# Queries and the first MLP layer in four column strips of the array, with one gelu and whole-array transposes

## The chip, the cores and the metric

The kernel runs on one core of one Trainium2 chip. The metric is the device time of one execution in microseconds (us), as a median of several. Each run is labelled fast or slow. All runs compared here are fast, except one single look (called contiguous below), whose state is unknown, and which is used only for the lengths of some matmuls.

"TensorE", "VectorE", "ScalarE" and "SyncE" are four engines of the core; in lines of the profile they are PE, DVE, ACT and SP. SPq is SyncE's queue, which here issues all the large loads, strictly in order.

## The reference

The result is one step of decoding: attention of 8 sequences over a cache, plus an MLP, plus the input.

```python
# B=8, Sq=1, D=640, H=32 heads (queries and K/V), Sk=4096, Dh=128, F=1728; all bf16
xn  = layernorm(x)
q   = (xn @ wq).reshape(B, 1, 32, 128)                 # wq: 640 x 4096
o   = softmax(q @ k_cache^T * Dh**-0.5) @ v_cache      # k_cache, v_cache: 8 x 32 x 4096 x 128
h   = gelu(layernorm(xn) @ w1 + b1)                    # w1: 640 x 1728, gelu by tanh
out = x + o.reshape(B, 1, 4096) @ wo + h @ w2 + b2
```

The two caches are 2 x 268 MB; all weights together are 14.9 MB. Everything is read once.

## The kernel before

The work is cut into 64 tiles: four heads of one sequence each, with 4.19 MB of K and 4.19 MB of V. There are two K buffers and two V buffers in SBUF. Tiles count from 0 here, loads in words: the first K is that of tile 0, the fifth K that of tile 4.

Every instruction has a position, and each engine executes its own in that order. Waits follow from what an instruction reads and writes. wq, w1 and the hidden layer `h` borrow the space of the two V buffers ("arena"):

```python
arena = KV_sb[:, NK:NK + NV, :]...          # the two V buffers
wq_sb, w1_sb, h_sb, b1_sb = ...             # all inside arena
# ... cut ...
for t in range(T):                          # T = 64
    pos = (-100.0, -98.0)[t] if t < NK else t - 1.5            # K of tile t
    ld(pos, kview(t), A_k_cache ..., [("K", t % NK, q) ...])
    pos = (0.45, 1.2)[t] if t < NV else t + 0.6                # V of tile t
    R = (["wqfree"], ["wqfree", "w1free", "hfree"])[t] if t < NV else []
    ld(pos, vview(t), A_v_cache ..., [("V", t % NV, q) ...], R)
```

So SyncE issues K0, wq, K1, w1, w2 at once. V0 waits until the queries have read wq. K2 waits until buffer 0 has been read. V1 waits until the hidden layer has been transposed out of the arena. K3 stands behind V1.

The two stages that the change rewrites, one matmul output of 8 rows at a time:

```python
def queries(n):                              # n = 0..7, four heads each
    def pe(e):                               # 5 matmuls 8 x 512
        for kc in range(DC):
            i = e.matmul(TRF[0:B, it.box[0], 0:HT * P], xnT_sb[:, 0, kc, :], wq_sb[:, kc, s], ...)
    add("pe", pos, pe, R=["wq", "xT0"], W=[it, "wqfree"], X=[it])
    add("act", pos + .01, lambda e: e.activation(qrow, TRF[0:B, ...], ACT.Copy), ...)     # 8 x 512
    def pe_t(e):                             # 4 transposes of 8 x 128
        for a in range(HT): i = e.transpose(...)
    # ... cut: copy into qT_sb ...

def hidden(n):                               # n = 0..3, 432 columns each
    def pe(e):
        for kc in range(DC):
            e.matmul(TRF[0:B, it.box[0], 0:FW], xnT_sb[:, 1, kc, :], w1_sb[:, kc, s], ...)
        return e.matmul(TRF[0:B, ...], ones_bf[0:1, 0:B], b1_sb[:, s], start=False, stop=True)
    add("act", pos + .001, ... e.activation(h_sb[:, s], TRF[0:B, ...], ACT.Gelu_apprx_tanh) ...)

def hidden_t():                              # 14 small transposes, two copies; W=[..., "hfree"]
    for j in range(FC):
        e.transpose(TR_ps[...], h_sb[:, j:FC * P:FC], ident_bf[0:B, 0:B])
# ... cut ...
add("pe", 1.04, pe_mlp2, ...)                # second MLP layer, 28 matmuls
add("dve", 1.94, ... xb2 += mlp ...)         # its sum, ahead of tile 2's work (2.0 on)
add("pe", c - 0.715, ... transpose of the row maxima ...)   # first softmax (c = 2): 1.285
```

The scores of a tile are made in two ways at once: a quarter of the keys on TensorE (transpose, copy, matmul), three quarters on VectorE, in two halves, each a product, a half-width sum and a reduction.

## Time and profile before

| | before |
|---|---|
| time, median of the first three runs | 1294.43 us (1293.76 to 1295.58) |
| profiled span | 1292.5 us |
| DMA rate from 100 to 1280 us | 431 GB/s |
| VectorE busy | 87% of the span |
| second V issued | 64.88 us |
| last V byte, then end of the span | 1287.94 us, 4.6 us later |

First the page of the kernel before: the span, the rate of the DMA in 40 equal slices (32 us each), and the chain of waits that ended last by engine.

```profile
span 1292.5 us, 19701 instructions
...
GB/s 406 412 413 429 427 434 432 432 426 433 432 433 433 426 431 433 432 429 428 433 433 430 433 426 435 430 433 430 431 430 433 429 431 431 433 428 432 425 437 338
...
DMA 77%; PE 10%; DVE 8%; issue 3%; ACT 1%; SPq 0%; DVEq 0%
...
```

The rate is the same everywhere but in the first three slices and the last. The chain is mostly DMA. This kernel waits for memory, and an improvement has to be looked for where memory waits for the kernel.

The same in chosen stretches. The columns are the stretch, its length, then busy us of PE, PEld, DVE, ACT and POOL with instruction counts, the granted clock of TensorE, the busy share of the DMA engines, and GB/s.

```profile
...
core 0: us, PE busy (x) PEld busy (x) DVE busy (x) ACT busy (x) POOL busy (x), PEclk, DMA share, GB/s
...
64.00:68.00 4.00, 3.60 (x24) 2.11 (x24) 0.30 (x1) 0.31 (x2) 0.00 (x0) 0.58 0.73 256
60.00:80.00 20.00, 12.87 (x107) 7.27 (x106) 13.09 (x8) 9.60 (x27) 0.00 (x0) 0.76 0.93 387
...
84.00:88.00 4.00, 2.24 (x30) 0.78 (x18) 3.96 (x2) 0.60 (x1) 0.00 (x0) 0.86 0.93 393
...
100.00:1280.00 1180.00, 591.28 (x7244) 376.07 (x7248) 1047.48 (x519) 460.59 (x1157) 0.00 (x0) 0.54 1.00 431
...
```

From 64 to 68 us the rate falls to 256 GB/s. The cause is in SyncE's issues, in order of time (start, length, what; x2 are two loads merged into one row, the second issued at the end of it, 84.07 us):

```profile
...
43.38 0.34 SPq L365 DMA_DIRECT2D KV_sb<-in_A_v_cache_dram  x1
47.77 0.33 SPq L365 DMA_DIRECT2D KV_sb<-in_A_k_cache_dram  x1
64.88 0.33 SPq L365 DMA_DIRECT2D KV_sb<-in_A_v_cache_dram  x1
65.25 19.18 SPq L365 DMA_DIRECT2D KV_sb<-in_A_k_cache_dram  x2
```

and in what SyncE waited for in the first 110 us (total, times, longest):

```profile
...
SPq L365 <- PE TR_ps L718: 16.8, 1, 16.8
...
```

The last transposes of the hidden layer (line 718) held the second V back by 16.8 us, and the fourth K stood behind it.

And the end, on TensorE: the last 32 value matmuls, which start when the last V piece has landed, and the output projection. Then two microseconds of the end in the table of stretches (the granted clock is the third number from the right).

```profile
...
1287.98 0.65 PE L626 MATMUL PV_ps<-KV_sb,P_sb 128*4 128x128 bf16 x32 [0.45 <-DMA KV_sb<-in_A_v_cache_dram]
...
1289.50 0.45 PE L665 MATMUL TR_ps<-wo_sb,oTn_sb 128*8 128x160 bf16 x16 [0.26 <-DVE oTn_sb L657]
```

```profile
...
1288.00:1290.00 2.00, 1.26 (x49) 0.78 (x49) 0.17 (x1) 0.28 (x1) 0.00 (x0) 1.00 0.00 0
...
```

The clock is 1.00 there (0.85 on the mean of the two microseconds before), and the 32 matmuls take 0.65 us.

### The profile page before, as it was taken

The numbers are of one execution on the slowest core, as the hardware profiler recorded it, in microseconds if no ns is written. First come the engines' busy times: TensorE is split into PE (matmuls) and PEld (weight loads), VectorE is DVE, ScalarE is ACT, GpSimd is POOL, SyncE is SP. The second block draws the span as 40 slices with busy tenths as digits, with TensorE's granted clock in tenths as the row PEclk, the third lists the DMA queues.
The fourth block names the chain that finished last, engine by engine and source line by source line (L and its number), as shares of the span: only waits on it lengthen the run. The fifth ranks groups of instructions, "written<-read, shape, count | busy, mean of one in ns | idle before, by whom it ended". The sixth has DMA issues, their size and how long they took to land.

```text
span 1292.5 us, 19701 instructions
## 1 busy us (share of the span) xinstructions
PE 653.1 (51%) x7852; PEld 407.0 (31%) x7853; DVE 1121.9 (87%) x586; ACT 500.6 (39%) x1248; POOL 0.2 (0%) x4
## 2 busy tenths in 40 slices
PE   2764454554454455454445444444544554455456
PEld 0343233333233233233233232232332332333332
DVE  4979999998898888998988988988888988889885
ACT  1553444334344234343243442443432443433432
POOL 0000000000000000000000000000000000000000
PEclk9865655555555555555555555655555555555566
DMA  9999999999999999999999999999999999999997
GB/s 406 412 413 429 427 434 432 432 426 433 432 433 433 426 431 433 432 429 428 433 433 430 433 426 435 430 433 430 431 430 433 429 431 431 433 428 432 425 437 338
DMA packets 23519, 551.99 MB, mean 427 GB/s; under 512 B 2297, under 2 KB 6481, under 8 KB 6482
## 3 DMA queue, kind: packets, MB, share of 16 engines
q1 hardware_dynamic: 23472, 551.80, 99.6%
q8 instruction: 7, 0.11, 0.0%
q10 hardware_dynamic: 34, 0.02, 0.0%
q14 instruction: 6, 0.05, 0.0%
HBM read 551.80 MB, written 0.01 MB: 427 GB/s over the span
## 4 chain that ended last, share of the span: by engine, by line
DMA 77%; PE 10%; DVE 8%; issue 3%; ACT 1%; SPq 0%; DVEq 0%
DMA KV_sb<-in_A_v_cache_dram 76%; PE PV_ps L616 8%; DVE Y_sb L544 4%; DVE Y_sb L548 2%; DMA KV_sb<-in_A_wq_dram 2%; DVE S_sb L551 1%; PE TR_ps L452 1%; PE TR_ps L704 0%; ACT KT_sb L515 0%; PE PV_ps L731 0%; ACT qrow_sb L456 0%; PE TR_ps L512 0%; PE TR_ps L705 0%; PE CH_ps L565 0%; PE S_ps L522 0%
## 5 line engine op out<-in xcount | busy, mean ns | idle before, releaser
L544 DVE TENSOR_TENSOR Y_sb<-KV_sb,qbc_sb 128x6144 bf16<-128x6144 bf16 x128 | 429.0, 3352 | 86.7 <-DMA KV_sb<-in_A_k_cache_dram 70.6
L551 DVE TENSOR_REDUCE S_sb<-Y_sb 128x48 f32<-128x3072 bf16 x128 | 429.2, 3353 | 4.4
L515 ACT ACTIVATE KT_sb<-TR_ps 128x1024 bf16<-128x1024 bf16 x256 | 254.3, 1019 | 223.6 <-PE TR_ps L512 222.1
L616 PE MATMUL PV_ps<-KV_sb,P_sb 128*16 128x512 bf16 x2040 | 226.8, 624 | 139.9 <-DMA KV_sb<-in_A_v_cache_dram 139.9
L512 PE MATMUL TR_ps<-ident_bf,KV_sb 128*128 128x128 bf16 x2048 | 247.4, 307 | 68.6 <-DMA KV_sb<-in_A_k_cache_dram 68.6
L548 DVE TENSOR_TENSOR Y_sb<-Y_sb 128x3072 bf16<-128x3072 bf16 x128 | 225.0, 1758 | 4.4
L512 PEld LDWEIGHTS TR_ps<-ident_bf,KV_sb 128*128 128x128 bf16 x2048 | 199.5, 141 | 79.2 <-DMA KV_sb<-in_A_k_cache_dram 73.1
L522 PE MATMUL S_ps<-qk_sb,KT_sb 128*128 128x4 bf16 x2048 | 98.2, 170 | 139.7 <-ACT KT_sb L515 138.0
L635 ACT ACTIVATE E_sb<-PV_ps 128x512 bf16<-128x512 f32 (+1 forms) x65 | 38.5, 592 | 319.9 <-PE PV_ps L616 318.4
L616 PEld LDWEIGHTS PV_ps<-KV_sb,P_sb 128*16 128x16 bf16 x2040 | 62.6, 124 | 253.0 <-DMA KV_sb<-in_A_v_cache_dram 145.5
L522 PEld LDWEIGHTS S_ps<-qk_sb,KT_sb 128*128 128x128 bf16 x2048 | 86.4, 109 | 170.5 <-ACT KT_sb L515 170.5
L583 ACT ACTIVATE P_sb<-S_sb,NB_sb 32x128 bf16<-32x128 f32 x256 | 101.9, 398 | 3.8
L641 PE MATMUL C_ps<-sel_bf,E_sb 128*128 128x4 bf16 x256 | 17.0, 172 | 135.4 <-DVE rinv_sb L597 112.4
L577 ACT ACTIVATE NB_sb<-CH_ps 128x2 f32<-128x2 f32 (+1 forms) x33 | 5.7, 172 | 167.1 <-PE CH_ps L573 167.1
L565 PE MATMUL CH_ps<-ident_f,M_sb 128*2 128x128 f32 (+1 forms) x33 | 12.1, 366 | 109.9 <-DVE M_sb L563 109.9
L641 PEld LDWEIGHTS C_ps<-sel_bf,E_sb 128*128 128x128 bf16 x256 | 11.5, 104 | 167.0 <-DVE rinv_sb L597 111.5
L532 ACT ACTIVATE S_sb<-S_ps 32x32 f32<-32x32 f32 x256 | 48.1, 188 | 32.2 <-PE S_ps L522 30.0
L583 ACT ACTIVATION_READ_ACCUMULATOR P_sb<-S_sb,NB_sb 32x1 f32 x256 | 47.0, 184 | 0.0
L565 PEld LDWEIGHTS CH_ps<-ident_f,M_sb 128*2 128x2 f32 (+1 forms) x33 | 2.6, 80 | 112.8 <-DVE M_sb L563 112.6
L656 DVE MEMSET oTn_sb<- 128x16 uint32 x31 | 2.2, 72 | 31.1 <-PE ACC_ps L676 31.1
L567 DVE TENSOR_REDUCE M_sb<-CH_ps 2x4 f32<-2x128 f32 (+1 forms) x33 | 9.2, 279 | 21.6 <-PE CH_ps L565 21.6
L594 PEld LDWEIGHTS C_ps<-rs_sb,ones_f 128*128 128x128 f32 x64 | 13.8, 269 | 25.1 <-issue 21.7
(91 smaller groups left out, 218.4 us busy)
## 6 DMA issues: line engine op xcount, KB each, us to landing
KV_sb<-in_A_k_cache_dram SPq DMA_DIRECT2D x64, 4096.0 KB, 26.8
KV_sb<-in_A_v_cache_dram SPq DMA_DIRECT2D x63, 4096.0 KB, 35.2
KV_sb<-in_A_wq_dram SPq DMA_DIRECT2D x1, 5120.0 KB, 24.1
wo_sb<-in_A_wo_dram SPq DMA_DIRECT2D x8, 640.0 KB, 30.9
KV_sb<-in_B_w_dram SPq DMA_DIRECT2D x1, 2160.0 KB, 38.0
w_sb<-in_B_w_dram SPq DMA_DIRECT2D x1, 2080.0 KB, 42.8
KV_sb<-in_A_v_cache_dram SPq DMA_DIRECT2D x1, 2048.0 KB, 12.6
KV_sb<-in_A_v_cache_dram SPq DMA_DIRECT2D x2, 1024.0 KB, 15.1
```

The source lines that it names most:

```text
L512: r = e.transpose(TR_ps[:, it.box[0], jj * P:(jj + 1) * P], kv[:, n * BK + jj, :], ident_bf[:, :])
L515: add("act", t - 0.59 + 0.12 * n, lambda e: e.activation(KT_sb[:, m % NS, :, :].rearrange("p a b -> p (a b)"), TR_ps[:, it.box[0], :], ACT ...
L522: r = e.matmul(S_ps[:, c:c + HT], KT_sb[:, m % NS, jj, :], qk_sb[:, :, i], start=True, stop=True)
L532: r = e.activation(S_sb[s, g % SR, i, 0:JP], S_ps[s, 0:JP * HT].rearrange("p (j a) -> p j a", a=HT)[:, :, a], ACT.Copy)
L544: return e.tensor_tensor(y, kv[:, j0:j1, :], qbc_sb[:, g % 2, i, :][:, None, :].to_broadcast([P, nj, P]), ALU.mult)
L548: lambda e, y=y, y2=y2: e.tensor_tensor(y2, y[:, :, 0:P // 2], y[:, :, P // 2:P], ALU.add),
L551: lambda e, y2=y2, j0=j0, j1=j1: e.tensor_reduce(S_sb[:, g % SR, i, j0:j1], y2, AX.X, ALU.add),
L565: add("pe", c - 0.715, lambda e: e.transpose(M1T_ps[0:n, :], M1_sb[:, 0:n], ident_f[:, :]), R=["M1", "identf"], W=["M1T"], X=["CH"])
L583: r = e.activation(P_sb[s, i, :, a, :], S_sb[s, g % SR, i, :].rearrange("p (m c) -> p m c", c=4), ACT.Exp, bias=NB_sb[s, g % 2, i:i + 1], ...
L616: r = e.matmul(PV_ps[32 * ct:32 * ct + HT * 4, t % 2, :], P_sb[:, i, m, :, :].rearrange("p a c -> p (a c)"), vv[:, 4 * m:4 * m + 4, :].rea ...
L635: add("act", pos, lambda e: e.activation(E_sb[:, k, 0:n], PV_ps[:, k, 0:n], ACT.Copy), R=[("PV", k)] + ["wo"] * (t % GT), W=[("E", k)], X= ...
L641: r = e.matmul(OT_i, E_sb[:, t % 2, c * P:(c + 1) * P], sel_bf[:, c:HT * 4:4], start=(c == 0), stop=(c == 3 and not last))
```

## The change

The intent is to use all of TensorE's array where only 8 of its 128 columns were used. Four heads of queries go to four strips of 32 output partitions in one PSUM tile, so one eviction of 128x128 and one whole transpose replace an eviction of 8x512 and four transposes. The hidden layer goes into four strips likewise: one gelu of 128x512 for four of 8x432, and four whole transposes for 14 small ones. To give the second layer its layout, the matmuls now read w1 three elements at a time in steps of 13.

```diff
 def pe(e):                                                       # queries
+    q = TRF[:, it.box[0], 0:P]
+    e.matmul(q, zeros_bf[:, :], zeros_bf[:, :], start=True, stop=False, ...)
     for kc in range(DC):
-        i = e.matmul(TRF[0:B, it.box[0], 0:HT * P], xnT_sb[:, 0, kc, :], wq_sb[:, kc, s], ...)
+        for a in range(HT):
+            h = n * HT + a
+            i = e.matmul(q[32 * a:32 * a + B, :], xnT_sb[:, 0, kc, :], wq_sb[:, kc, h * P:(h + 1) * P], ...)
...
-    for a in range(HT):
-        i = e.transpose(TR_ps[:, it2.box[0], a * B:(a + 1) * B], qrow[:, a * P:(a + 1) * P], ident_bf[0:B, 0:B])
+    e.transpose(TR_ps[:, it2.box[0], 0:P], qrow, ident_bf[:, :])
...
-for n in range(FB):
-    hidden(n)                                                    # 6 matmuls and a gelu each
-hidden_t()
+w13 = w1_sb[:, :, 0:FC * P].rearrange("p c (f u) -> p c f u", u=FC)
+for k in range(FB):
+    yield k, 0, FS, w13[:, :, :, 3 * k:3 * k + 3], ...           # 384 columns, strip k
+yield 0, FS, FS + P, w13[:, :, :, FC - 1], ...                   # 128 columns, strip 0
+yield 1, FS, FS + FR, w1_sb[:, :, FC * P:F], ...                 # 64 columns, strip 1
...
+e.matmul(h, zeros_bf[:, :], ...)                                 # zero, then 36 matmuls
+e.activation(h_sb, TRF[:, it_h.box[0], :], ACT.Gelu_apprx_tanh)  # one gelu, 128 x 512
+for c in range(3):
+    e.transpose(TR_ps[:, it_t.box[0], c * P:(c + 1) * P], h_sb[:, c:FS:3], ident_bf[:, :])
```

The order of the loads is not touched.

## The prediction

> **What bounds the kernel now: the DMA queue, almost everywhere.** The busy table of stretches gives a mean DMA share of 1.00 at 431 GB/s from 80 to 1280 us; 551.8 MB at that rate are 1280 us of the 1292.5 us span. The chain that ended last is 77% DMA. VectorE (87% busy) needs 2 x (3.35 + 1.76 + 3.35) = 16.9 us per tile, whose K and V take 8.39 MB / 431 GB/s = 19.5 us to load: slack. Time can only come from DMA holes, or from the 4.6 us tail after the last V byte (1287.9 us), which the change leaves alone.
>
> **Where the DMA starves.** By 20 us stretches: 401 (start latency), 416, 421, 387 GB/s, then about 431. The hole is at 64 to 67 us (107, 229, 262 GB/s): everything queued (18.05 MB at start, first V, third K: 26.4 MB, dry at about 63 us) was used up while the second V tile waited at the head of SyncE's in-order queue for the hidden-layer transposes (that wait: 16.8 us; issued 64.88 us). Against 431 GB/s, 60 to 80 us lost 0.88 MB, 2.0 us; 62 to 68 alone lost 1.3 us. A small loss (0.3 us) lies at 44 to 48 us, where the first V was issued at 43.38 us, just as the queue ran out.
>
> **Costs of the change.**
> - Queries, before: groups 3 to 7 repeat every 1.92 us: five 8x512 matmuls 1.26, eviction 0.59, semaphores. After: one zeroing matmul and 20 matmuls 8x128 in four strips. The trace's own strip matmuls give the rate: 32 of 16x512 in 3.59 us, 112 ns each against a 427 ns pitch unpacked (first query group); 32 of 4x128 in 0.65 us. The Trainium skill (TensorEngine Tiling, Theoretical Speedup: up to 4x for a dimension up to 32) agrees: 3.8x here. Estimate: matmuls 0.55, eviction of 128 columns 0.29 (as the 128x128 eviction at 1288.7), 0.95 us per group. Queries end near 36 us, not 44.3.
> - Hidden layer, before: 55.23 to 65.2 us. After: zeroing 0.43, six passes of 384 + 128 columns, about 0.43 each at the low clock, one gelu 0.6 for four of 0.52, four transposes 0.4, one copy 0.3: about 5 us. The weights are now read in 26-byte steps; the Trainium skill (SBUF — State Buffer, Specifications: 16-byte cachelines) says that crossing lines pays a penalty; nothing in this trace measures it. Even doubled, it ends earlier.
>
> **Effect.** First V issued near 35.5 us, third K near 40, hidden from about 47, second V near 52, fourth K near 57 to 60: all ahead of the dry point near 63 us, by about 10 us. The hole goes. Later the DMA never starves, so nothing more can be won: some 12 us off TensorE and ScalarE become about 2.1 us (2.0 + 0.3, less noise): 1292.3 us, 0.16% faster. Range 1290.3 to 1294.6.
>
> **What would show it.** SyncE's issues at these times; 60 to 80 us at 420 GB/s or more; query period near 1 us; tail 4.6 us; 431 GB/s after 80 us.
>
> **What would make it wrong.** Strided weight reads slow enough (over 15 us) to keep the hole; the four strips not overlapping; a new hole later because K and V issues shift against each other; a steady rate that moves by 0.2%, the whole effect. Over 2% would need 26 us of DMA holes, which do not exist.

## More of the kernel before

On VectorE, around the first softmax and tile 2 (start, length, instruction, in brackets its idle time before and what ended it):

```profile
...
71.07 0.28 DVE L567 TENSOR_REDUCE M_sb<-CH_ps 2x4 f32<-2x128 f32 x1 [6.77 <-PE CH_ps L565]
...
80.45 3.35 DVE L544 TENSOR_TENSOR Y_sb<-KV_sb,qbc_sb 128x6144 bf16<-128x6144 bf16 x1
...
```

VectorE idled 6.77 us for a small transpose of the maxima, which stood behind the hidden layer and the second MLP layer on TensorE. The row of 80.45 us is the second product of tile 2, the last reader of the third K on VectorE. It ended at 83.80, and the fifth K was issued at 84.07.

## The result, and the profile after

| | before | after |
|---|---|---|
| time, median of 6 runs each | 1294.53 us | 1293.23 us |
| range | 1293.76 to 1295.58 | 1292.5 to 1293.3 |
| ratio | | 0.9988, 95% interval 0.9975 to 1.0001 |
| profiled span | 1292.5 us | 1291.2 us |
| last V byte | 1287.94 us | 1285.97 us |
| from there to the end | 4.6 us | 5.2 us |

A ratio here is the mean time of one kernel's fast runs over that of the other's fast runs of the same rounds, so it is not quite the ratio of the medians quoted. Its interval just reaches 1; two repeats below gave 0.9987 (0.9974 to 1.0001) and 0.9985 (0.9972 to 0.9999), and no timed run of the changed kernel was as slow as the fastest of before of the same rounds.

The page after:

```profile
span 1291.2 us, 19910 instructions
...
GB/s 407 423 427 427 435 429 431 433 429 427 434 430 431 428 434 427 434 431 427 430 434 430 432 427 431 430 434 430 427 432 431 431 433 428 429 432 430 429 435 329
...
DMA 83%; PE 8%; DVE 7%; issue 2%; ACT 0%; SPq 0%; DVEq 0%
...
```

The second and third slice rose from 412 and 413 GB/s to 423 and 427. The stretches:

```profile
...
core 0: us, PE busy (x) PEld busy (x) DVE busy (x) ACT busy (x) POOL busy (x), PEclk, DMA share, GB/s
...
64.00:68.00 4.00, 1.62 (x16) 1.62 (x16) 1.65 (x1) 3.93 (x13) 0.00 (x0) 0.53 1.03 442
60.00:80.00 20.00, 9.75 (x108) 5.82 (x109) 17.00 (x10) 10.82 (x28) 0.00 (x0) 0.66 0.99 424
...
100.00:1280.00 1180.00, 588.20 (x7256) 374.51 (x7256) 1044.47 (x517) 461.08 (x1158) 0.00 (x0) 0.56 1.00 431
...
```

The hole at 64 to 68 us is gone (442 GB/s for 256), 60 to 80 us moves at 424 for 387, and the rate from 100 us on is the same 431. SyncE's issues and its wait for the hidden layer (line 726 now), as before:

```profile
...
36.01 0.34 SPq L365 DMA_DIRECT2D KV_sb<-in_A_v_cache_dram  x1
40.81 0.33 SPq L365 DMA_DIRECT2D KV_sb<-in_A_k_cache_dram  x1
53.64 0.33 SPq L365 DMA_DIRECT2D KV_sb<-in_A_v_cache_dram  x1
56.91 21.88 SPq L365 DMA_DIRECT2D KV_sb<-in_A_k_cache_dram  x2
...
```

```profile
...
SPq L365 <- PE TR_ps L726: 12.5, 1, 12.5
...
```

The second V went out 11.2 us earlier. The fifth K, merged into the last row, went out at 78.44 us instead of 84.07. VectorE, around the first softmax and tile 2:

```profile
...
62.88 0.28 DVE L567 TENSOR_REDUCE M_sb<-CH_ps 2x4 f32<-2x128 f32 x1 [0.36 <-PE CH_ps L565]
...
74.81 3.35 DVE L544 TENSOR_TENSOR Y_sb<-KV_sb,qbc_sb 128x6144 bf16<-128x6144 bf16 x1
...
```

The small transpose came after 0.36 us of idling, not 6.77. The end, on TensorE and in the clock:

```profile
...
1286.02 1.06 PE L626 MATMUL PV_ps<-KV_sb,P_sb 128*4 128x128 bf16 x32 [0.43 <-DMA KV_sb<-in_A_v_cache_dram]
...
1287.95 0.70 PE L665 MATMUL TR_ps<-wo_sb,oTn_sb 128*8 128x160 bf16 x16 [0.26 <-DVE oTn_sb L657]
```

```profile
...
1286.00:1288.00 2.00, 1.30 (x37) 0.93 (x41) 0.17 (x1) 0.28 (x1) 0.00 (x0) 0.50 0.00 0
...
```

The stretch of 1286 to 1288 us, in which the 32 matmuls ran, has a clock of 0.50. The last data came 2.0 us earlier, but the same 32 matmuls took 1.06 us instead of 0.65 and the projection 0.70 instead of 0.45, at half the clock. In this pair of profiles that gave back 0.7 us; whether the change is to blame is taken up below.

The stages themselves: the queries ran from 25.2 to 36.6 us (25.3 to 44.3 before), the hidden layer from 48.2 to 53.9 us (55.2 to 65.2 before). That is 11.8 us less (7.5 and 4.3), for 2.0 us at the last byte and 1.3 us at the end.

### The profile page after: what moved, and what is told of

It reads as the page before. It is cut to its first block, busy times and chain, and to the rows that moved or that the text cites. A ratio compares the mean times of both kernels' runs of the same rounds, so it can differ in the third digit from the quotient of the medians.

```text
span 1291.2 us, 19910 instructions
## 1 busy us (share of the span) xinstructions
PE 640.8 (50%) x7958; PEld 406.5 (31%) x7960; DVE 1122.2 (87%) x586; ACT 497.1 (39%) x1244; POOL 0.2 (0%) x4
## 4 chain that ended last, share of the span: by engine, by line
DMA 83%; PE 8%; DVE 7%; issue 2%; ACT 0%; SPq 0%; DVEq 0%
DMA KV_sb<-in_A_v_cache_dram 78%; PE PV_ps L616 8%; DVE Y_sb L544 4%; DMA KV_sb<-in_A_k_cache_dram 2%; DMA KV_sb<-in_A_wq_dram 2%; DVE Y_sb L548 2%; DVE S_sb L551 1%; SPq L365 0%; PE PV_ps L626 0%; DVE M_sb L563 0%; PE CH_ps L565 0%; PE TR_ps L665 0%; PE TR_ps L456 0%; PE CH_ps L478 0%; DVE rinv_sb L597 0%
## 5 line engine op out<-in xcount | busy, mean ns | idle before, releaser
L616 PE MATMUL PV_ps<-KV_sb,P_sb 128*16 128x512 bf16 x2040 | 223.1, 616 | 144.2 <-DMA KV_sb<-in_A_v_cache_dram 144.2
L676 PE MATMUL ACC_ps<-oTn_sb,wo_sb 128*128 128x8 bf16 x620 | 21.5, 169 | 0.0
```

The costliest lines, as they stand in the source:

```text
L616: r = e.matmul(PV_ps[32 * ct:32 * ct + HT * 4, t % 2, :], P_sb[:, i, m, :, :].rearrange("p a c -> p (a c)"), vv[:, 4 * m:4 * m + 4, :].rea ...
L676: r = e.matmul(ACC_ps[:, c * B:(c + 1) * B], wo_sb[:, a, c * P:(c + 1) * P], oTn_sb[:, a, :], start=False, stop=False, skip_group_check=True)
```

## The experiments

Twelve kernels were run. All but one gave correct results. The theory was the prediction's: the whole gain is the DMA hole at 64 to 67 us, which lasted until the second V was issued. The rival was that the gain comes from the work taken off TensorE and ScalarE as such. The dry point of a queue is the time at which everything issued so far has been moved; a load issued after it leaves a hole, and it is the deadline for that issue. A summary first (the medians come from different rounds and chips, so compare kernels by the ratios); "last V byte" is the start of the last 32 value matmuls less 0.04 us of issue, as the chain of waits gives it, and "tail" is the profiled span less that.

| kernel | second V issued | fifth K issued | last V byte | tail | time, median | ratio to before |
|---|---|---|---|---|---|---|
| before | 64.88 | 84.07 | 1287.94 | 4.6 | 1294.53 | 1 |
| after | 53.64 | 78.44 | 1285.97 | 5.2 | 1293.23 | 0.9988 |
| after, repeat 1 | 53.78 | 78.48 | 1285.84 | 5.3 | 1293.15 | 0.9987 |
| after, repeat 2 | 53.86 | 78.51 | 1286.08 | 5.2 | 1293.12 | 0.9985 |
| loads reordered (e1) | 65.06 | 84.32 | 1288.00 | 5.2 | 1295.04 | 1.0006 |
| new queries only (e2) | 57.28 | 78.77 | 1286.32 | 5.3 | 1293.18 | 0.9987 |
| new hidden only (e3) | 59.17 | 78.84 | 1286.06 | 5.2 | 1293.54 | 0.9992 |
| second V held, short (e4) | 63.83 | 78.87 | 1287.13 | 4.6 | 1294.13 | 0.9996 |
| second V held, long (e5) | 69.01 | 78.50 | 1292.42 | 5.2 | 1299.36 | 1.0036 |
| reordered, softmax first (e8) | 63.84 | 79.70 | 1286.32 | 5.2 | 1293.56 | 0.9990 |
| softmax first (e9) | 63.78 | 79.83 | 1287.18 | 5.2 | 1294.19 | 0.9997 |
| warm tail (e7) | 53.86 | 78.57 | not seen | | 1292.49 | 0.9983 |
| light warm tail (e10) | 53.70 | 78.53 | 1286.25 | 4.6 | 1292.48 | 0.9980 |

### The change repeated

No edit.

> The changed kernel unchanged, for the spread: last V byte at 1286.0 us within 0.3, ratio to before 0.9988 with a narrower interval. The tail after that byte was 4.6 us before (granted clock 1.0 there) and 5.2 after (0.5). If the tail's clock is chance, it may be either here; if the change set it, 5.2 again.

> The changed kernel once more, on the same chip as the other three: ratio 0.9987, last V byte 1286.0, tail 5.2 us.

Measured: last V byte 1285.84 and 1286.08 us, tails 5.3 and 5.2 us, ratios 0.9987 (interval 0.9974 to 1.0001) and 0.9985 (0.9972 to 0.9999). All three profiles of the changed kernel agree within 0.25 us in the last byte, and all three have the half clock in the tail. The profiles of e1 and e4 below show that this isn't proof that the change set it.

### One half of the change each (e2, e3)

The edits are the two halves of the diff above, each alone.

> The new queries with the old hidden layer. Hole theory: second V issued near 57.5 us, still ahead of the dry point at about 64 us, so the full gain: last V byte at 1286.0 us, ratio 0.9985. Rival (gain in proportion to the work taken off, 7.4 of 11.2 us of lead): 1286.7 us.

> The new hidden layer with the old queries. Hole theory: second V issued near 60.8 us, just ahead of the dry point: most of the gain, last V byte at 1286.3 us (the 0.3 us loss at 44 to 48 us stays), ratio 0.9987. Rival (in proportion to work): 4.6 of 11.2 us of lead, 1287.2 us.

Measured: last V byte 1286.32 and 1286.06 us, ratios 0.9987 (0.9973 to 1.0) and 0.9992 (0.9978 to 1.0005). Each half alone brings nearly the whole gain, 1.6 and 1.9 us of 2.0. e2 by itself decides nothing: 1286.32 us lies about midway between the 1286.0 of the theory and the 1286.7 of the rival. But the gains of the halves don't add, and the half that took less work off (the hidden layer) isn't the lesser one in the last byte: 1286.06 us, where the rival had 1287.2. That fits a deadline and speaks against the rival.

### The second V held back in the changed kernel (e4, e5)

```diff
-pos = (0.45, 1.2)[t] if t < NV else t + 0.6
-R = (["wqfree"], ["wqfree", "w1free", "hfree"])[t] if t < NV else []
+pos = (0.45, 1.345)[t] if t < NV else t + 0.6
+R = (["wqfree"], ["wqfree", "w1free", "hfree", ("Pt", 1)])[t] if t < NV else []
```

(e5; e4 has `("NB", 0)`, an earlier event, in its place.)

> The changed kernel with the second V load also waiting for the first softmax's maxima (an ACT copy that ended at 63.7 us), the same work on every engine. Hole theory: issue at about 63.8 us, the hole comes back in part: last V byte about 1.0 us later than 1285.97, ratio of it to before 0.9995. Rival (work, not issue time): same as the changed kernel, 1285.97.

> As e4, but waiting for the exponentials of the second tile (ended at 69.0 us). Hole theory: issue at about 69.2 us, each microsecond past the dry point is lost: last V byte 5.5 to 6.5 us later than in the changed kernel, about 1292 us, time 1298.5 to 1299.5, hole in the rate from 64 to 71 us. Rival: no difference from the changed kernel, 1293.2.

Measured: the second V was issued at 63.83 and 69.01 us, the last V byte came at 1287.13 and 1292.42 us: 1.2 and 6.5 us later than in the changed kernel. Between the two, 5.2 us of delay cost 5.3 us. The work of the engines is the same in both, so the rival is out. Extrapolating back at one for one from e4 to the 1285.97 us of the changed kernel gives a deadline for the second V of about 62.7 us (an estimate from these numbers). The rate around the hole of e5, in stretches of 1 us:

```profile
...
66.00:67.00 1.00, 0.56 (x6) 0.56 (x7) 0.58 (x1) 0.97 (x5) 0.00 (x0) 0.50 0.00 0
...
70.00:71.00 1.00, 0.81 (x14) 0.82 (x15) 1.00 (x1) 1.00 (x2) 0.00 (x0) 0.50 1.61 459
...
```

All four stretches from 65 to 69 us show 0: nothing moves until the load is issued, and the rate is back within two microseconds after.

### Only the order of the loads changed, in the kernel before (e1)

```diff
-pos = (0.45, 1.2)[t] if t < NV else t + 0.6
+pos = (0.45, 1.55)[t] if t < NV else t + 0.6
```

> The kernel before, with one number changed: the second V load stands behind the fourth K load in SyncE's order, so that K goes out as soon as its buffer is free (about 58.7 us) and fills the hole. No strips. Hole theory (the whole gain of the change is the DMA hole at 64 to 67 us): the last V byte lands at 1286.0 us instead of 1287.94, 60 to 80 us moves at 420 GB/s or more, ratio to before 0.9985. Rival (the gain comes from less work on TensorE and ScalarE at the start): lands at 1287.9, ratio 1.000.

Measured: 1295.04 us, ratio 1.0006 (0.9992 to 1.0019), last V byte 1288.00 us. Of this expectation, only the rate from 60 to 80 us came true (425 GB/s); the last byte and the ratio came out as the rival had them, and only e8 below decides between the rival and a second hole. The loads (the fourth K went out at the end of the first row, near 58.8 us) and the rate:

```profile
...
47.89 11.25 SPq L365 DMA_DIRECT2D KV_sb<-in_A_k_cache_dram  x2
...
84.32 0.35 SPq L365 DMA_DIRECT2D KV_sb<-in_A_k_cache_dram  x1
...
```

```profile
...
core 0: us, PE busy (x) PEld busy (x) DVE busy (x) ACT busy (x) POOL busy (x), PEclk, DMA share, GB/s
...
64.00:68.00 4.00, 3.60 (x24) 2.17 (x25) 0.41 (x1) 0.31 (x2) 0.00 (x0) 0.62 0.96 412
...
84.00:88.00 4.00, 2.52 (x30) 0.96 (x22) 3.93 (x3) 0.60 (x1) 0.00 (x0) 0.82 0.86 287
...
```

The hole at 64 us was filled, as meant, and a new one opened at 84 to 88 us (287 GB/s for 393 in before). With the first hole filled, the queue ran dry about two microseconds sooner, and the fifth K could not go out sooner: it was issued at 84.32 us, 0.3 us after VectorE had finished the second product of tile 2. VectorE was late because it had idled 6.91 us for the small transpose behind the hidden layer and the second MLP layer, as in before. So the kernel before has two deadlines in a row, and misses both by about as much. In its own trace the second hardly shows (393 GB/s from 84 to 88 us), because the first miss pushes the second deadline back.

### Both deadlines met without the change (e8), and the second alone (e9)

e9 puts the first softmax's small matmuls ahead of the second MLP layer on TensorE, and that layer's sum behind the first half of tile 2 on VectorE. e8 has the reordered loads of e1 as well.

```diff
-pos = (0.45, 1.2)[t] if t < NV else t + 0.6                     # e8 only
+pos = (0.45, 1.55)[t] if t < NV else t + 0.6                    # e8 only
-add("pe", 1.04, pe_mlp2, ...)
+add("pe", 1.32, pe_mlp2, ...)
-add("dve", 1.94, ... xb2 += mlp ...)
+add("dve", 2.035, ... xb2 += mlp ...)
-add("pe", 1.95, pe_zero, ...)
+add("pe", 2.036, pe_zero, ...)
-    return 2.0 + i                       # position of tile i's value matmuls
+    return 2.0 + i + 0.04 * (i == 0)
```

> The kernel before, no strips: as e1, and the first softmax's small transposes stand ahead of the second MLP layer on TensorE, the sum of that layer behind the first third of tile 2's work on VectorE. e1 filled the hole at 64 us but got one at 84 to 87, because the fifth K load waits for VectorE's second product of tile 2, which was held up (6.9 us of idle) by the old hidden layer and the second MLP layer. Two-hole theory: with both mended the fifth K goes out near 79 us instead of 84.3, both holes are gone, last V byte at 1286.0 us, ratio to before 0.9985, all without the change. If e1 failed for another reason (the order itself): 1288 us, ratio 1.000.

> Only the second half of e8: softmax ahead of the second MLP layer, loads in the old order. Two-hole theory: fifth K near 79 us, but the hole at 64 to 67 us stays as in before, since the second V is still issued at 64.9: last V byte 1287.9 us, ratio 1.000. If the start of tile 2 on VectorE were what counts: 1286.0 us.

Measured for e8: last V byte 1286.32 us, ratio 0.9990 (0.9976 to 1.0003). The fifth K and the rates:

```profile
...
63.84 0.33 SPq L365 DMA_DIRECT2D KV_sb<-in_A_v_cache_dram  x1
79.70 0.36 SPq L365 DMA_DIRECT2D KV_sb<-in_A_k_cache_dram  x1
...
```

```profile
...
core 0: us, PE busy (x) PEld busy (x) DVE busy (x) ACT busy (x) POOL busy (x), PEclk, DMA share, GB/s
...
64.00:68.00 4.00, 3.26 (x20) 1.60 (x21) 1.69 (x3) 2.65 (x9) 0.00 (x0) 0.50 1.02 436
...
84.00:88.00 4.00, 2.96 (x36) 2.70 (x37) 3.97 (x4) 2.03 (x3) 0.00 (x0) 0.51 1.03 442
...
```

Neither hole is left (436 and 442 GB/s). Without a strip, with 8x512 matmuls and four gelus, the loads of before are 1.6 us sooner at the end, of the 2.0 that the change brings (what the other 0.35 us is wasn't tested). The second V may even go out at 63.84 us here, since the fourth K was already queued ahead of it.

Measured for e9: last V byte 1287.18 us, ratio 0.9997 (0.9983 to 1.001). I had expected 1287.9. The difference is explained by the same rule: the second V was issued at 63.78 us in this profile, not 64.88. At that time e4 lost the same (63.83 us and 1287.13 us). Meeting the second deadline alone brings nothing beyond what the second V's own time gives.

### Weights read in contiguous runs (e6)

```diff
-yield k, 0, FS, w13[:, :, :, 3 * k:3 * k + 3], ...
+yield k, 0, FS, w1_sb[:, :, FS * k:FS * k + FS], ...
-yield 0, FS, FS + P, w13[:, :, :, FC - 1], ...
+yield 0, FS, FS + P, w1_sb[:, :, 4 * FS:4 * FS + P], ...
```

The result is wrong (relative error 0.034): the hidden units come in another order than the second layer expects.

> The changed kernel with the first-layer weights read in runs of 384 contiguous elements instead of three at a time in steps of 13 (wrong hidden order, wrong result on purpose). A pass of one contraction chunk took 0.57 us after, where 512 columns at the low clock make 0.43. If the strided reads cost the difference: 0.43 us a pass and hidden 0.8 us shorter. If not: 0.57 again. The time stays at the changed kernel's either way, since second V is issued ahead of the dry point.

Measured: the five passes over the chunks of the contraction, and then the one for the bias. First the changed kernel, then this one, both at a granted clock of 0.50:

```profile
...
48.77 2.90 PE L716 MATMUL TR_ps<-KV_sb,xnT_sb 128*8 128x384 bf16 x30 [0.38 <-issue]
51.60 0.70 PE L716 MATMUL TR_ps<-KV_sb,ones_bf 1*8 1x384 bf16 x6
...
```

```profile
...
48.63 2.29 PE L716 MATMUL TR_ps<-KV_sb,xnT_sb 128*8 128x384 bf16 x30 [0.38 <-issue]
50.85 0.58 PE L716 MATMUL TR_ps<-KV_sb,ones_bf 1*8 1x384 bf16 x6
...
```

From the start of the passes to the start of the bias pass it is 2.83 us for the strided reads and 2.22 us for contiguous ones, so 0.57 and 0.44 us a pass, a cost of 28%, or 0.61 us over the five. The bias is read in the same way; from the start of the passes to the gelu it is 0.72 us less here (2.85 us for 3.57). 512 columns in the estimate of the prediction made 0.43. The one run took 1293.17 us, and the last V byte came at 1286.14 us: no difference, as expected for work that is ahead of its deadline.

### Matmuls of no use in the tail (e7, e10)

```diff
+warm(p0 - 0.005, 2, vview(t - 1), ...)     # n matmuls 128x512 of the identity with V data,
+warm(p0 + 0.065, 1, vv, ...)               # into a PSUM bank that nobody reads any more;
+warm(p0 + 0.105, 2, vv, ...)               # e7 has 2, 3, 2 of them, e10 has 2, 1, 2
```

> The changed kernel with seven matmuls of no use, 128x512, put into TensorE's waits for the last V pieces. If the granted clock in the tail follows how busy TensorE was in the microseconds before: clock 1.0 at 1286 to 1289 us, the last 32 value matmuls 0.65 us instead of 1.06, tail 4.5 us instead of 5.2, ratio to before 0.9983. If chance: clock 0.5, tail 5.2, ratio 0.9988. If they get in the way: tail over 5.2.

> As e7 with one idle matmul instead of three in the second place, since the three ran at the low clock and held up the last value matmuls until 0.7 us after their data. If the clock still rises: tail after the last V byte 4.6 us, time 0.3 us below e7's, ratio to before 0.9980. If five matmuls are too few to raise it: tail 5.2 us, ratio 0.9987 as the changed kernel.

Measured for e7: 1292.49 us, ratio 0.9983 (0.9969 to 0.9997). In its profile the clock rose to 1.00 only near 1285 us. The three matmuls in the second place ran at the low clock, and the last value matmuls started at 1286.70 us, held up by the added work and not by data. So the tail can't be read off, and the profiled span was 1291.2 us, as in the changed kernel; the profiled run was the slowest of its five.

Measured for e10: 1292.48 us (1292.32 to 1292.59, five runs), ratio 0.9980 (0.9966 to 0.9993). On the same chip the changed kernel took 1293.12 us (1292.9 to 1293.57, five runs), so no run of one reaches the other. TensorE's last matmuls and the clock:

```profile
...
1286.29 0.65 PE L626 MATMUL PV_ps<-KV_sb,P_sb 128*4 128x128 bf16 x32 [0.87 <-DMA KV_sb<-in_A_v_cache_dram]
...
1287.81 0.45 PE L677 MATMUL TR_ps<-wo_sb,oTn_sb 128*8 128x160 bf16 x16 [0.26 <-DVE oTn_sb L669]
```

```profile
...
1286.00:1288.00 2.00, 1.02 (x45) 0.75 (x49) 0.17 (x1) 0.28 (x1) 0.00 (x0) 1.00 0.00 0
...
```

The clock is 1.00 here (and in the stretches of two microseconds on either side), the 32 matmuls take 0.65 us again and the projection 0.45, and the tail is 4.6 us. e10 is faster than both kernels, by 0.6 us than the changed one. The other forecast, 0.3 us below e7's time, missed: 1292.48 us for 1292.49 (on another chip).

What makes the clock rise or fall is only in part seen. Both profiles have it at 1.00 from 1281 to 1282 us. In the changed kernel TensorE was then idle from 1282.1 to 1283.6 us, waiting for the next piece of V, and the clock fell at 1282.80 us. In e10 it was kept busy in part of that time, and the clock stayed. But this is one profile of each, and the clock has a timing of its own. In the clock records of each of the fourteen traces it changes only on a fixed grid of 3.41 us (to within 0.001 us), and where the grid lies against the work differs from execution to execution. That the added matmuls pay is shown by the times of five runs each, not by this pair.

## Why the prediction was right

The time was in the stated range (1290.3 to 1294.6), though by the medians 1.3 us were won where about 2.1 was forecast. Most of the steps held:

- **What bounds the kernel.** "The DMA queue, almost everywhere" held: 11.8 us off the engines gave 2.0 us at the last byte, and 431 GB/s from 100 us on stayed as it was.
- **The hole and its size.** 2.0 us + 0.3 us was the forecast for the last byte, 2.0 us was measured. The 0.3 us isn't seen: e3, which moved only 385 GB/s from 44 to 48 us, ended within 0.1 us of the changed kernel. e5 shows the mechanism at full size: one microsecond for each that the second V is late.
- **The strips.** Queries ended at 36.6 us (forecast 36), first V at 36.01 (35.5), third K at 40.81 (40), hidden from 48.2 (47), second V at 53.64 (52), fourth K at 56.91 (57 to 60). The trace had strip matmuls of its own, and they gave the rate: 3.8 times, where the Trainium skill (TensorEngine Tiling (Array Packing), Theoretical Speedup) says up to 4. The changed kernel agrees: a set of four matmuls of 128 columns starts every 107 ns, where one of 512 columns took 427 ns in the first groups before: 4.0 times. Both ran at half clock, to judge by their lengths.
- **A period of 0.95 us a query group** was too short: 1.31 us was measured. The term that was mis-sized is the matmul part, "0.55": the zeroing matmul takes 0.22 us before the first strip starts (29.81 to 30.03), and the 20 matmuls 0.70 until the last is done. That is 0.92 us ahead of an eviction of 0.28. What the forecast missed is the clock. Most of these matmuls last 311 ns, as the last value matmuls do at a clock of 0.50 (219 ns at 1.00). The first rise of the clock on record in this trace is at 40.34 us, after the queries. Before, it is at 33.90 us, ahead of groups 3 to 7, whose period the forecast took as its measure. (The table of stretches prints 1.00 where a trace has no clock record yet, so it can't be used for this stage.) It did not matter: the end came 0.6 us after the forecast (the third group followed the second at 0.85 us, as the two have a buffer each), and the second V had 9 us to spare.
- **Strided reads.** The prediction left the penalty open; e6 measured it: 0.61 us over the weights, 0.72 us with the bias.

Two steps were not right, and the runs put others in their place:

- **"the 4.6 us tail after the last V byte (1287.9 us), which the change leaves alone".** What failed is 4.6 us as a fixed term. The tail was 5.2 to 5.3 us in all three profiles of the changed kernel, but also 5.2 us in e1, e8 and e9, which have no strip, and 4.6 us in e4, which has them all. Of the twelve profiles without added matmuls only those of before and e4 have the short tail. In the 5 us ahead of its last data TensorE did the same work in the first repeat as in before, with the same pauses to 0.02 us, and yet the clock rose to 1.00 at 1286.59 us in before and stayed at 0.50 here. First before, then the repeat:

```profile
...
1285.54 1.03 PE L616 MATMUL PV_ps<-KV_sb,P_sb 128*16 128x512 bf16 x8 [0.56 <-DMA KV_sb<-in_A_v_cache_dram]
...
```

```profile
...
1283.45 1.03 PE L616 MATMUL PV_ps<-KV_sb,P_sb 128*16 128x512 bf16 x8 [0.57 <-DMA KV_sb<-in_A_v_cache_dram]
...
1285.88 1.06 PE L626 MATMUL PV_ps<-KV_sb,P_sb 128*4 128x128 bf16 x32 [0.43 <-DMA KV_sb<-in_A_v_cache_dram]
...
```

  So the 0.67 us, of 1.97 won, that went there in the two profiles compared are not shown to be the change's. The forecast started from an execution with a short tail, which looks like chance (two of twelve had it). How often each kernel has it is open, since the other runs have no profile. The medians of the rounds with the two repeats are 1.75 and 2.27 us apart, where the first six runs each gave 1.3 us. e10 shows that the short tail can be had in the changed kernel.
- **"The hole is at 64 to 67 us: ... while the second V tile waited"**, as the only hole. That was true of the trace, but not of the kernel. e1 filled it and gained nothing, since the fifth K was then too late by as much itself. The change got the gain because it brought both forward: the second V by 11.2 us, and, by ending VectorE's wait behind the MLP, the fifth K by 5.6 us. e8 brings both forward by other means and has most of the gain without a strip, and e9 shows that the second alone isn't enough. The prediction names a later hole only as a risk, and says that later "the DMA never starves". That the change met the second deadline too was luck, as far as its reasoning goes.

## What to carry to other kernels

In a kernel bound by its loads, a faster stage is worth only what it moves the issue of a load from after the queue's dry point to before it; work out that point from bytes and rate, then look which wait holds the next load, and the one after it. Filling one hole in a trace can open the next, because the first delay hides the second deadline: test the fill alone before crediting it. After the last byte no load hides anything, and there the clock of TensorE counts; a few idle matmuls in the last waits were worth 0.6 us here, where the whole change was worth 1.3 to 2.3 us.

## What the Trainium skill lacked or had wrong

- TensorE: Matmul & The Clock Gate, the tables of Part 1 and of "Why this matters for your kernels": two clocks, half after an idle window of about 3.4 us, and the advice to allow no pauses of more than about 3 us. The two clocks are seen here (0.50 and 1.00), and so is the free-running window of Part 1: every change lies on a grid of 3.41 us. But no idle window was needed: in the tail of the changed kernel the clock fell at 1282.80 us, after a window in which TensorE had been busy for 53% (1.80 of 3.42 us), 0.7 us into a pause of 1.4 us. The page has no busy share below which the clock falls, or above which it rises. In the light warm tail it held after a window with 63% (2.15 of 3.42 us). These shares are rough, since the trace models the ends of matmuls, and they give no sharp limit for the rise: it rose after a window with 83% in before (at 1286.59 us), but not after one with 83% in the contiguous run (at 1284.57 us).
- SBUF — State Buffer, Specifications: the 16-byte cachelines and a penalty for crossing them are stated, its size isn't. For TensorE's moving operand, three bf16 elements at a time in steps of 26 bytes, in four strips at half clock, the whole cost of the stride was 28%: 0.57 us a pass for 0.44 us. How much of it is the crossing of lines wasn't isolated.
- DMA: Bandwidth & Descriptors, Specifications, gives about 358 GB/s as the limit of one core's HBM bandwidth. One core alone read 431 GB/s here for 1180 us. HBM Reference, Specifications, says that a core streaming alone is well above that share, about 425 GB/s, and this agrees to 1.4%. The first page has 425 GB/s too, as a single-core figure further down; its row of the limit should say that it is the share of a core whose neighbour streams as well.
- No page says that a load held back at the head of an in-order queue costs one for one past the queue's dry point and nothing before it (5.2 us later, 5.3 us lost, in the long hold).
